# The second attention block put behind the first 24 products of the first MoE in TensorE's order

## The chip, the cores and the metric

The kernel runs on one core of a Trainium2 chip. The metric is the device time of one execution in microseconds; less is better. The times shown are medians over several executions, and the profile is of one further execution.

## What is computed

Attention with a decay over four batches, eight heads, 576 positions and a head dimension of 64, then two feed-forward layers over the 2304 tokens, all in float32 precision. The reference, cut to what matters:

```python
scores = matmul(q, k.T) / sqrt(64)
cum = cumsum(log(clip(f, 1e-4, 1)), -1)
scores = where(causal, -1e9, scores + cum[..., :, None] - cum[..., None, :])
attn = softmax(scores)                    # over keys, with 1e-9 in the divisor
x = matmul(attn, v) -> [2304, 512]        # tokens by heads*dim
h = x @ w_in                              # [512, 2048]
x = maximum(0.01 * h, h) @ w_out          # [2048, 512]
return ((x @ w_a) * (x @ w_b)) @ w_out2   # 512 -> 1536 -> 512
```

## The kernel before, in words

The attention runs in eight blocks (b, r): for batch b, r = 0 takes the first 256 queries and r = 1 the last 320. Each block goes through its eight heads in pairs. For the first batch, TensorE transposes queries and keys (tq, tk; ScalarE copies them out as qn, kn), makes the scores (s, and s4 for the last 64 queries), VectorE adds the decay and takes the maximum (p, line 320), ScalarE takes the exponential (line 291), TensorE transposes the result (pp; ScalarE copies it out as ph) and multiplies it with the values (av). The output is normalised (xn), transposed once more (px), and split into a high part xh (ScalarE) and a low part xl (VectorE) that are the input of the first MoE layer.

The first MoE layer goes over chunks of 256 tokens, and in each over eight pairs of 128 features. `l1(i, pr)` makes 24 products for chunk i and pair pr: two feature tiles, four slices of the model dimension, and three products each (high by high, high by low, low by high), into one PSUM tile `h`. For all chunks but the last two there is one such PSUM tile; the av and px of the first attention block use it too. ScalarE then reads it twice (gh and hs, the activation), VectorE makes gl = hs − gh, and `l2` makes 24 products into the two tiles `y`. `work(i, pr)` calls `l1` and then the `l2` of the pair before it.

The weights come from HBM as pairs of 32-bit words of doubles. For each 128-wide piece (wi_0 to wi_15 of w_in, wo_0 to wo_15 of w_out) `load_weight` issues one DMA on SP's queue into a raw buffer, of which there are two; then ScalarE takes the absolute value (L94), VectorE assembles a float in four steps (L95, L96, L97, L100; L97 and L100 read the raw buffer), ScalarE rounds it to the high part (L87), and VectorE subtracts to get the low part (L88).

The kernel is written in Tile. A scheduler orders the instructions of every engine by its own estimate of when each is ready and by priorities; the order in which the code is written sets the priorities, and `tc.high_priority` moves some ahead. The whole order of every engine is fixed before the kernel runs. The first block of attention (`att_steps(0)`) is written first, then the first two pieces of work of chunk 0 with a high priority, then the second block (`att_steps(1)`, the last 320 queries of batch 0) with loads and more work of chunk 0 between its steps. The names of the rows below carry these indices: s_0_1_0_2 is a score of block (0, 1), head 0, key tile 2; h_0_1 is chunk 0, pair 1; c_wi_6 and raw_wi_6 belong to the load of wi_6.

Of the kernel before, what the change touches and what calls it, by code (L numbers as in the profile page):

```python
# [26 lines left out]
def kernel(  # L27
# [13 lines left out]
    nc = tc.nc  # L41
# [5 lines left out]
    NF1, NF2, ND = F1 // P, F2 // P, DM // P  # L47
# [34 lines left out]
    def f32(ap):  # L82
        return ap.bitcast(F32)
# [77 lines left out]
    def x_chunk(c):  # L161
        if c not in xh:
            pool, bufs = (late["p"], 1) if c % 3 == 2 else (mp, 2)
            xh[c] = pool.tile([P, HP, T1], F32R, tag="xh", bufs=bufs, name=f"xh_{c}")
            xl[c] = pool.tile([P, HP, T1], F32R, tag="xl", bufs=bufs, name=f"xl_{c}")
        return xh[c], xl[c]
# [390 lines left out]
    def load_a(fi):  # L557
        wa[fi] = (
            *load_weight(wpool, stage, cols(w_in, fi), f"wi_{fi}", 512, 2, bufs=4 * NF1),
            *load_weight(wpool, stage, rows(w_out, fi), f"wo_{fi}", 512, 2, bufs=4 * NF1),  # L560
        )

    def l1(i, pr):
        ch, cl = x_chunk(i)
        last = i >= NB1 - 2
        hps = (pools["ps_ab"] if last else ps_y).tile(
            [P, 2, T1], F32, tag="ab0" if last else "h", bufs=2 if last else 1, name=f"h_{i}_{pr}"
        )
        for u in range(2):
            wih, wil = wa[2 * pr + u][0], wa[2 * pr + u][1]  # L570
            n = 0
            for c in reversed(range(ND)):
                for w, x in ((wih, ch), (wih, cl), (wil, ch)):
                    nc.tensor.matmul(  # L574
                        hps[:, u, :], w[:, c * P : c * P + P], x[:, c, :], start=(n == 0), stop=(n == 3 * ND - 1)
                    )
                    n += 1

        hs = mp.tile([P, 2, T1], F32, tag="hs", name=f"hs_{i}_{pr}")
        gh = mp.tile([P, 2, T1], F32R, tag="gh", name=f"gh_{i}_{pr}")  # L580
        gl = mp.tile([P, 2, T1], F32R, tag="gl", name=f"gl_{i}_{pr}")
        with tc.high_priority(offset=1):
            nc.scalar.activation(gh, hps, AF.Prelu, alpha=0.01)
            nc.scalar.activation(hs, hps, AF.Prelu, alpha=0.01)
        with tc.high_priority(offset=400 if last else 0):
            nc.vector.tensor_tensor(out=gl, in0=hs, in1=f32(gh), op=ALU.subtract)  # L586
        return gh, gl
# [3 lines left out]
    def l2(i, pr, gh, gl):  # L591
        if pr == 0:
            pool, tag, bufs = (pools["ps_ab"], "ab1", 2) if i == NB1 - 1 else (ps_y, "y", 2)
            ybank[i] = [pool.tile([P, 2, T1], F32, tag=tag, bufs=bufs, name=f"y_{i}_{z}") for z in range(2)]
        for u in range(2):
            fi = 2 * pr + u
            woh, wol = wa[fi][2], wa[fi][3]
            for d in range(ND):
                o = ybank[i][d // 2][:, d % 2, :]
                for n, (w, g) in enumerate(((woh, gh), (woh, gl), (wol, gh))):  # L600
                    nc.tensor.matmul(  # L601
                        o, w[:, d * P : d * P + P], g[:, u, :],
                        start=(fi == 0 and n == 0 and d % 2 == 0),
                        stop=(fi == NF1 - 1 and n == 2 and d % 2 == 1),
                    )
        if pr == NF1 // 2 - 1:
            for z in range(2):
                yo = mp.tile([P, 2, T1], F32, tag="hs", name=f"yo_{i}_{z}")
                nc.scalar.copy(yo, ybank[i][z])
                nc.scalar.dma_start(  # L610
                    y_dram[2 * z : 2 * z + 2, :, i * T1 : i * T1 + T1].rearrange("u p t -> p u t"), yo
                )
# [74 lines left out]
    def att_steps(n):  # L687

        if n == 0:

            sts = [{} for _ in range(H)]
            scores = [att_scores(*blocks[n], h, sts[h]) for h in range(H)]
            values = [att_values(*blocks[n], h, sts[h]) for h in range(H)]
            before = None
            for h in range(0, 2):
                next(scores[h])
            for h in range(0, H, 2):
                for z, _ in enumerate(beside(beside(*scores[h : h + 2]), before)):
                    if z == 3:
                        for g in scores[h + 2 : h + 4]:  # L700
                            next(g)
                    yield
                before = chain(*values[h : h + 2])
            yield from before
            return
        second = None
        for h in range(H):
            st = {}
            yield from beside(att_scores(*blocks[n], h, st), second)
            second = att_values(*blocks[n], h, st)  # L710
            if h % 2 == 1 and blocks[n][1] == 1:
                second = chain(second, att_last(blocks[n][0], h // 2, st["rec4"]))
        yield from second

    def chain(a, b):
        yield from a
        yield from b

    def beside(a, b):
        while a or b:  # L720
            for g in (a, b):
                if g and next(g, "end") == "end":
                    if g is a:
                        a = None
                    else:
                        b = None
                else:
                    if g:
                        yield
# [3 lines left out]
    def work(i, fi):  # L733
        pend.append((i, fi, *l1(i, fi)))
        if len(pend) > 1:
            l2(*pend.pop(0))


    zero, one = ([(i, fi) for fi in range(NF1 // 2)] for i in range(2))
    loaded = 0  # L740

    def load_next():
        nonlocal loaded
        if loaded < NF1:
            load_a(loaded)
            loaded += 1
# [7 lines left out]
        load_next()  # L754
    with tc.high_priority(offset=2000):
        work(*zero.pop(0))
        work(*zero.pop(0))
    for s, _ in enumerate(att_steps(1)):
        if s % 8 == 7:
            load_next()  # L760
        if s % 16 == 15 and 2 * (NF1 // 2 - len(zero)) + 2 <= loaded:
            work(*zero.pop(0))
    while zero:
        load_next()
        load_next()
# [80 lines left out]
```

## Time and profile before

| what | value |
|---|---|
| median of 3 runs | 1111.56 us (1110.79 to 1111.98) |
| profiled execution | 1109.59 us |
| its span (first to last instruction) | 1107.8 us |
| mean granted clock of TensorE | 0.989 of full speed |
| busy share of the span: TensorE, VectorE, ScalarE, GpSimd | 97%, 55%, 49%, 18% |

The profiled execution is 1.97 us under the median of the runs. Of its own time 1.8 us lie outside the span. Busy time is that of instructions only: an engine that waits is idle, and one that works at a lower clock is busy for longer. The profile lists for each group of instructions the idle time ahead of it and what ended that.

### The profile page before, as it was taken

Reading aid. Unit: us, or ns where it says so; the run is one execution under the profiler, and the core shown is the slowest. Engines: PE = TensorE matmul, PEld = TensorE weight load, DVE = VectorE, ACT = ScalarE, POOL = GpSimd, SP = SyncE. Lnnn points to the kernel's source line nnn. Section 1 sums busy time; section 2 is a strip of 40 time slices with the busy share of each in tenths; the row PEclk is TensorE's granted clock in tenths of the full one; section 3 lists DMA queues with packets and bytes.
Section 4 is the critical chain, followed back from the end, with each engine's and each line's share of the span. In section 5 each row is a group of like instructions: output and inputs, shape, how many; then the busy total and the mean of one; then the engine's idle time right before and its main releaser. Section 6 shows DMA issues by size and latency. Waiting matters only on the chain.

```text
span 1107.8 us, 19615 instructions
## 1 busy us (share of the span) xinstructions
PE 1079.2 (97%) x7021; PEld 967.2 (87%) x7021; DVE 614.0 (55%) x1484; ACT 543.2 (49%) x1257; POOL 204.5 (18%) x434
## 2 busy tenths in 40 slices
PE   5899999999999999999999999999999999999998
PEld 3577779999999999999999997888888888888897
DVE  5869887887777777677478877412111211211122
ACT  4656668878787878768554454312111211211121
POOL 4423322434243432333000000102001000100000
PEclk9879999999999999999999999999999999999999
DMA  7645545442452334422054454202000100100010
GB/s 196 195 130 172 159 120 103 96 94 48 79 124 62 94 58 83 109 62 53 9 165 144 142 152 152 76 1 76 1 1 20 48 1 1 48 1 1 1 39 20
DMA packets 185729, 86.77 MB, mean 78 GB/s; under 512 B 143840, under 2 KB 173536, under 8 KB 185632
## 3 DMA queue, kind: packets, MB, share of 16 engines
q1 hardware_dynamic: 180736, 80.80, 28.6%
q10 hardware_dynamic: 4896, 4.72, 1.3%
q8 instruction: 56, 0.92, 0.4%
q14 instruction: 41, 0.34, 0.1%
HBM read 75.96 MB, written 9.51 MB: 77 GB/s over the span
## 4 chain that ended last, share of the span: by engine, by line
PE 72%; DMA 11%; DVE 8%; ACT 4%; issue 3%; SPq 1%; POOL 0%; ACTq 0%; DVEq 0%; POOLq 0%
PE ab L653 25%; PE o L676 13%; PE h L574 11%; PE y L601 10%; PE s L76 5%; PE av L76 5%; PE pp L76 3%; DMA raw_wa<-in_moe_w_a_dram 3%; DMA raw_wb<-in_moe_w_b_dram 2%; DMA raw_wc<-in_moe_w_out_dram 1%; DMA xq<-in_q_dram 1%; DMA cumb<-cum_dram 1%; DMA raw_wi<-in_moe_w_in_dram 1%; DMA raw_wo<-in_moe_w_out_dram 1%; DMA sy<-y_dram 1%
## 5 line engine op out<-in xcount | busy, mean ns | idle before, releaser
L659 DVE TENSOR_TENSOR p<-ab,p 128x512 f32<-128x512 f32 (+1 forms) x60 | 38.3, 638 | 274.6 <-PE ab L653 272.0
L574 PE MATMUL h<-xh,wi_hi 128*128 128x256 f32 x576 | 164.6, 286 | 1.2 <-ACT wi_hi L87 1.2
L574 PE MATMUL h<-xh,wi_lo 128*128 128x256 f32 x576 | 164.1, 285 | 0.9 <-DVE wi_lo L88 0.9
L574 PE MATMUL h<-xl,wi_hi 128*128 128x256 f32 x576 | 164.3, 285 | 0.0
L601 PE MATMUL y<-gl,wo_hi 128*128 128x256 f32 x576 | 161.7, 282 | 1.0 <-DVE gl L586 1.0
L601 PE MATMUL y<-gh,wo_lo 128*128 128x256 f32 x576 | 161.1, 282 | 0.0
L601 PE MATMUL y<-gh,wo_hi 128*128 128x256 f32 x576 | 159.4, 282 | 0.0
L658 ACT COPY p<-ab 128x512 f32<-128x512 f32 (+1 forms) x60 | 32.7, 544 | 169.1 <-PE ab L653 168.7
L574 PEld LDWEIGHTS h<-xh,wi_hi 128*128 128x128 f32 x576 | 109.8, 191 | 5.2 <-issue 2.3
L574 PEld LDWEIGHTS h<-xh,wi_lo 128*128 128x128 f32 x576 | 109.8, 191 | 2.5 <-DVE wi_lo L88 1.1
L601 PEld LDWEIGHTS y<-gl,wo_hi 128*128 128x128 f32 x576 | 108.4, 188 | 2.9 <-DVE gl L586 1.6
L574 PEld LDWEIGHTS h<-xl,wi_hi 128*128 128x128 f32 x576 | 109.8, 191 | 0.8 <-issue 0.4
L601 PEld LDWEIGHTS y<-gh,wo_lo 128*128 128x128 f32 x576 | 108.3, 188 | 1.7 <-issue 1.2
L601 PEld LDWEIGHTS y<-gh,wo_hi 128*128 128x128 f32 x576 | 107.3, 188 | 1.8 <-issue 0.8
L313 POOL TENSOR_SCALAR p<-cumb,ncum_t 128x384 f32<-128x384 f32 (+1 forms) x112 | 75.1, 678 | 162.4 <-PE pp L76 47.8
L87 ACT CAST pph<-p 128x512 fp32r<-128x512 f32 (+1 forms) x60 | 34.8, 580 | 126.3 <-DVE p L659 126.2
L291 ACT ACTIVATE p<-p,stat 128x384 f32<-128x384 f32 (+4 forms) x128 | 77.0, 603 | 34.5 <-DVE stat L320 27.2
L88 POOL TENSOR_TENSOR yl<-sy,yh 128x512 fp32r<-128x512 f32 (+1 forms) x16 | 19.2, 1211 | 393.7 <-ACT yh L87 393.6
L653 PE MATMUL ab<-yh,wb_hi 128*128 128x512 f32 (+1 forms) x240 | 88.3, 368 | 0.9 <-DVE p L659 0.6
L653 PE MATMUL ab<-yh,wa_hi 128*128 128x512 f32 (+1 forms) x240 | 88.1, 367 | 0.0
L653 PE MATMUL ab<-yh,wa_lo 128*128 128x512 f32 (+1 forms) x240 | 88.1, 367 | 0.0
L653 PE MATMUL ab<-yl,wa_hi 128*128 128x512 f32 (+1 forms) x240 | 88.1, 367 | 0.0
(168 smaller groups left out, 2612.6 us busy)
## 6 DMA issues: line engine op xcount, KB each, us to landing
cumb<-cum_dram SPq DMA_DIRECT2D x32, 288.0 KB, 3.9
raw_wi<-in_moe_w_in_dram SPq DMA_DIRECT2D x16, 512.0 KB, 4.0
raw_wo<-in_moe_w_out_dram SPq DMA_DIRECT2D x16, 512.0 KB, 4.0
raw_wa<-in_moe_w_a_dram SPq DMA_DIRECT2D x12, 512.0 KB, 3.5
raw_wb<-in_moe_w_b_dram SPq DMA_DIRECT2D x12, 512.0 KB, 3.5
raw_wc<-in_moe_w_out_dram SPq DMA_DIRECT2D x12, 512.0 KB, 3.6
xq<-in_q_dram SPq DMA_DIRECT2D x144, 32.0 KB, 2.0
y_dram<-yo ACTq DMA_DIRECT2D x18, 256.0 KB, 3.0
```

Source lines behind the costliest of these rows:

```text
L76: return method(*args, **kw)
L87: nc.scalar.copy(hi, src)
L88: (lo_engine or nc.gpsimd).tensor_tensor(out=lo, in0=src, in1=f32(hi), op=ALU.subtract)
L291: act_att.activation(pt, pt, AF.Exp, bias=stat[:, 0, s : s + 1], scale=-1.0, accum_out=stat[:, 1, s : s + 1])
L313: pool_att.tensor_scalar(pt, cumb[:, :n], 1.0, ncum_t[:, t, bh : bh + 1], op0=ALU.mult, op1=ALU.add)
L574: nc.tensor.matmul(hps[:, u, :], w[:, c * P : c * P + P], x[:, c, :], start=(n == 0), stop=(n == 3 * ND - 1))
L601: nc.tensor.matmul(o, w[:, d * P : d * P + P], g[:, u, :], start=(fi == 0 and n == 0 and d % 2 == 0), stop=(fi == NF1 - 1 and n == 2 and d ...
L653: nc.tensor.matmul(o[:, :tn], w[:, c * P : c * P + P], y[:, c, :tn], start=(m == 0), stop=(m == 3 * ND - 1))
L658: nc.scalar.copy(p[:, :tn], ab[0][:, :tn])
L659: nc.vector.tensor_tensor(out=p[:, :tn], in0=ab[1][:, :tn], in1=p[:, :tn], op=ALU.mult)
L676: nc.tensor.matmul(o, g[:, t * P : t * P + P], w, start=(fi == 0 and m == 0), stop=(fi == NF2 - 1 and m == 2))
```

## The change

The last product that `l1` issues is remembered in `end[0]`. After the first `work` of chunk 0 this is the last of the first 24 products, h_0_0. Everything that the following loop traces on TensorE, that is the second attention block and the work of chunk 0 that is written between its steps, is then placed in a context (`tc.issue_after`) that lets no TensorE instruction stand ahead of it in TensorE's order.

```diff
+    end = [None]
+
     def l1(i, pr):
...
-                    nc.tensor.matmul(
+                    end[0] = nc.tensor.matmul(
                         hps[:, u, :], w[:, c * P : c * P + P], x[:, c, :], start=(n == 0), stop=(n == 3 * ND - 1)
                     )
...
     with tc.high_priority(offset=2000):
         work(*zero.pop(0))
+        first_end = end[0]
         work(*zero.pop(0))
-    for s, _ in enumerate(att_steps(1)):
-        if s % 8 == 7:
-            load_next()
-        if s % 16 == 15 and 2 * (NF1 // 2 - len(zero)) + 2 <= loaded:
-            work(*zero.pop(0))
+    with tc.issue_after(first_end.ins if hasattr(first_end, "ins") else first_end):
+        for s, _ in enumerate(att_steps(1)):
+            if s % 8 == 7:
+                load_next()
+            if s % 16 == 15 and 2 * (NF1 // 2 - len(zero)) + 2 <= loaded:
+                work(*zero.pop(0))
```

The count of instructions on every engine stays the same. The scheduler orders all engines anew around this, so three orders show what moves.

The first place is TensorE around the first 24 products. Before, the rows ahead of them are these (tq, tk and pp are transposes, s and s4 scores; h_0_0 is the first MoE product):

```order
L76 MATMUL s_0_1_0_2_741<-kn_0_1_0_709,qn_0_1_0_708 128x384
L76 MATMUL s_0_1_0_3_750<-kn_0_1_0_709,qn_0_1_0_708 128x512
L76 MATMUL px_0_0_7_614<-ident_65,xn_0_0_7_587 128x128 x2
L76 MATMUL s4_0_1_0_0_760<-kn_0_1_0_709,qn_0_1_0_708 64x288
L76 MATMUL pp_0_1_0_0_807<-ident_65,p_0_1_0_2_736 128x128 x3
L76 MATMUL s4_0_1_0_1_763<-kn_0_1_0_709,qn_0_1_0_708 64x288
L76 MATMUL pp_0_1_0_1_813<-ident_65,p_0_1_0_3_745 128x128 x4
L76 MATMUL tq_0_1_2_935<-ident_65,xq_0_1_2_925 128x128 x2
L76 MATMUL tq_0_1_2_935<-ident_65,xk_0_1_2_926 128x64
L76 MATMUL tk_0_1_2_0_940<-ident_65,xk_0_1_2_926 128x128 x2
L76 MATMUL s_0_1_1_2_803<-kn_0_1_0_709,qn_0_1_0_708 128x384
L574 MATMUL h_0_0_619<-xh_0_309,wi_0_hi_185 128x256
```

After the change px_0_0_7 is followed at once by the 24 products, and these are the rows around their last one:

```order
L576 MATMUL h_0_0_619<-xl_0_310,wi_1_hi_260 128x256
L576 MATMUL h_0_0_619<-xh_0_309,wi_1_lo_261 128x256
L76 MATMUL tq_0_1_0_720<-ident_65,xq_0_1_0_710 128x128 x2
L76 MATMUL tq_0_1_0_720<-ident_65,xk_0_1_0_711 128x64
L76 MATMUL tk_0_1_0_0_725<-ident_65,xk_0_1_0_711 128x128 x2
L76 MATMUL tk_0_1_0_2_729<-ident_65,xk_0_1_0_711 128x128 x2
L76 MATMUL tk_0_1_0_2_729<-ident_65,xk_0_1_0_711 128x64
L603 MATMUL y_0_0_681<-gh_0_0_645,wo_0_hi_197 128x256
L603 MATMUL y_0_1_682<-gh_0_0_645,wo_0_hi_197 128x256
L576 MATMUL h_0_1_650<-xh_0_309,wi_2_hi_332 128x256
```

Before, the scores of the first two heads stood ahead of the first MoE products; now even the first transposes of the second block stand behind them, and its first scores behind h_0_1.

The second place is ScalarE around the activation of the first 24 products (gh_0_0, hs_0_0). Before:

```order
L94 ACTIVATE c_wo_5_0_548<-raw_wo_5_0_546 128x512
L218 COPY kn_0_1_2_924<-tk_0_1_2_0_940 128x256
L87 CAST wi_5_hi_532<-c_wi_5_0_536 128x512
L291 ACTIVATE p_0_1_1_2_798,stat_0_1_0_707<-p_0_1_1_2_798,stat_0_1_0_707 128x384
L583 ACTIVATE gh_0_0_645<-h_0_0_619 128x512
L584 ACTIVATE hs_0_0_644<-h_0_0_619 128x512
L94 ACTIVATE c_wi_6_0_594<-raw_wi_6_0_592 128x512
```

After the change:

```order
L94 ACTIVATE c_wi_5_0_536<-raw_wi_5_0_534 128x512
L76 CAST xh_0_309<-px_0_0_7_614 128x256
L94 ACTIVATE c_wo_5_0_548<-raw_wo_5_0_546 128x512
L87 CAST wi_5_hi_532<-c_wi_5_0_536 128x512
L94 ACTIVATE c_wi_6_0_594<-raw_wi_6_0_592 128x512
L87 CAST wo_5_hi_544<-c_wo_5_0_548 128x512
L585 ACTIVATE gh_0_0_645<-h_0_0_619 128x512
L586 ACTIVATE hs_0_0_644<-h_0_0_619 128x512
L208 ACTIVATE qn_0_1_0_708<-tq_0_1_0_720 128x320
L218 COPY kn_0_1_0_709<-tk_0_1_0_0_725 128x256
```

The activation now stands behind L94 of c_wi_6, which before came after it, and the copies qn and kn of the second block stand behind the activation.

The third place is VectorE around the first softmax of the second block (p_0_1_0_2). Before:

```order
L76 TENSOR_TENSOR xn_0_0_7_587<-av_0_0_7_580,rec_0_0_7_577 128x2x64 x2
L100 SCALAR_TENSOR_TENSOR c_wo_4_0_489<-raw_wo_4_0_487,c_wo_4_0_489 128x512
L320 ISA p_0_1_0_2_736,stat_0_1_0_707<-s_0_1_0_2_741,p_0_1_0_2_736 128x384
L320 ISA stat_0_1_0_707 128x1
L95 TENSOR_SCALAR c_wi_5_0_536<-c_wi_5_0_536 128x512
```

After the change:

```order
L95 TENSOR_SCALAR c_wo_6_0_606<-c_wo_6_0_606 128x512
L96 TENSOR_SCALAR c_wo_6_0_606<-c_wo_6_0_606 128x512
L88 TENSOR_TENSOR wi_6_lo_591<-c_wi_6_0_594,wi_6_hi_590 128x512
L97 SCALAR_TENSOR_TENSOR c_wo_6_0_606<-raw_wo_6_0_604,c_wo_6_0_606 128x512
L320 ISA p_0_1_0_2_736,stat_0_1_0_707<-s_0_1_0_2_741,p_0_1_0_2_736 128x384
L320 ISA stat_0_1_0_707 128x1
```

The softmax has moved behind the conversions of wi_5, wo_5, wi_6 and most of wo_6, and xn_0_0_7, which stood ahead of the last step of c_wo_4, now stands behind it.

## Rows read from the trace of the kernel before

**Rows 1.** Busy time, share of the span and instructions of each engine.

```profile
PE 1079.2 (97%) x7021; PEld 967.2 (87%) x7021; DVE 614.0 (55%) x1484; ACT 543.2 (49%) x1257; POOL 204.5 (18%) x434
```

**Rows 2.** Windows, all engines: stretch, length, busy (count), PEclk, DMA share, GB/s.

```profile
core 0: us, PE busy (x) PEld busy (x) DVE busy (x) ACT busy (x) POOL busy (x), PEclk, DMA share, GB/s
55.00:83.00 28.00, 27.59 (x144) 19.69 (x143) 18.70 (x47) 15.38 (x34) 6.54 (x9) 0.78 0.48 128
```

**Rows 3.** Windows of PE alone: stretch, length, busy (count), PEclk, DMA share, GB/s.

```profile
54.00:66.00 12.00, 11.98 (x37) 0.50 0.67 179
68.00:158.00 90.00, 89.16 (x603) 1.00 0.56 155
158.00:166.00 8.00, 5.75 (x34) 0.80 0.19 31
```

**Rows 4.** Timeline of PE: start, us, instruction, count, [idle before and its releaser].

```profile
52.65 2.40 PE L76 MATMUL s<-kn,qn 64*128 64x384 f32 x4
54.98 0.69 PE L76 MATMUL px<-ident,xn 128*128 128x128 f32 x2
55.60 1.22 PE L76 MATMUL s<-kn,qn 64*64 64x288 f32 x2
...
62.78 0.58 PE L574 MATMUL h<-xh,wi_hi 128*128 128x256 f32 x1
...
67.82 1.12 PE L76 MATMUL s<-kn,qn 64*128 64x512 f32 x2
...
70.56 0.28 PE L574 MATMUL h<-xh,wi_hi 128*128 128x256 f32 x1
...
73.24 0.28 PE L574 MATMUL h<-xh,wi_lo 128*128 128x256 f32 x1
...
161.10 0.39 PE L574 MATMUL h<-xh,wi_hi 128*128 128x256 f32 x1 [1.15 <-ACT wi_hi L87]
...
162.76 0.50 PE L574 MATMUL h<-xh,wi_lo 128*128 128x256 f32 x1 [0.92 <-DVE wi_lo L88]
```

**Rows 5.** Timeline of DVE around the conversions and the first scores.

```profile
53.42 0.69 DVE L100 SCALAR_TENSOR_TENSOR c_wo<-raw_wo,c_wo 128x512 int32<-128x512 int32 x1
54.02 0.56 DVE L320 CUSTOM_DVE_ANT_0 p<-s,p 128x384 f32<-128x384 f32 x1
...
55.70 0.43 DVE L95 TENSOR_SCALAR c_wi<-c_wi 128x512 f32<-128x512 f32 x1 [1.11 <-ACT c_wi L94]
...
57.97 0.41 DVE L76 TENSOR_TENSOR xl<-px,xh 128x256 fp32r<-128x256 f32 x1
58.30 0.67 DVE L97 SCALAR_TENSOR_TENSOR c_wi<-raw_wi,c_wi 128x512 int32<-128x512 int32 x1
...
63.00 0.56 DVE L320 CUSTOM_DVE_ANT_0 p<-s,p 128x384 f32<-128x384 f32 x1 [2.95 <-PE s L76]
...
69.09 0.69 DVE L320 CUSTOM_DVE_ANT_0 p<-s,p 128x512 f32<-128x512 f32 x1 [2.80 <-PE s L76]
```

**Rows 6.** Timeline of ACT around the loads and the first activations.

```profile
55.01 0.66 ACT L94 ACTIVATE c_wi<-raw_wi 128x512 f32<-128x512 f32 x1 [3.20 <-DMA raw_wi<-in_moe_w_in_dram]
55.57 0.60 ACT L87 CAST wo_hi<-c_wo 128x512 fp32r<-128x512 f32 x1
...
56.69 0.35 ACT L76 CAST xh<-px 128x256 fp32r<-128x256 f32 x1
...
67.93 0.60 ACT L583 ACTIVATE gh<-h 128x512 fp32r<-128x512 f32 x1 [3.62 <-PE h L574]
68.42 0.59 ACT L584 ACTIVATE hs<-h 128x512 f32<-128x512 f32 x1
...
75.16 0.66 ACT L94 ACTIVATE c_wo<-raw_wo 128x512 f32<-128x512 f32 x1 [3.44 <-DMA raw_wo<-in_moe_w_out_dram]
75.73 0.58 ACT L583 ACTIVATE gh<-h 128x512 fp32r<-128x512 f32 x1
```

**Rows 7.** Timeline of SP's queue: the loads of wi_5 and wi_6.

```profile
50.85 0.37 SPq L114 DMA_DIRECT2D raw_wi<-in_moe_w_in_dram  x1
...
61.39 0.40 SPq L114 DMA_DIRECT2D raw_wi<-in_moe_w_in_dram  x1
```

## The prediction

> **What bounds the kernel now.** The busy line of the page comes first: TensorE is busy 97% of the span, VectorE 55% [rows 1]. So the time can change through TensorE's idle time, through the clock granted to it, or through the work, and the work stays: no instruction is added or removed. The windows come next. TensorE is busy 27.59 of 28.00 us in 55 to 83 [rows 2]; over 68 to 158 it lacks less than 1 of 90 us and holds the full clock (1.00), while in 158 to 166 it lacks 2.25 of 8 us [rows 3]. TensorE's timeline names that place: the last pair of the first chunk waits 1.15 us for the cast of a weight and 0.92 us for its low part, which VectorE makes [rows 4]. [...]
>
> The other loss is a clock that is low while TensorE has work: 54 to 66 is busy for 11.98 of 12.00 us at 0.50 [rows 3]. That stretch holds scores, transposes and the first products of the first MoE.
>
> **The change, part by part.** Each term is a moment that shifts; the moments of the changed kernel are worked out from durations of rows.
>
> 1. *When the first 24 products (h0) begin.* They need the last piece of input: px (0.69 [rows 4]), xh on ScalarE, xl on VectorE. Before, px ran at 54.98 behind scores, and h0 at 62.78 behind more of the second block [rows 4]. Now px needs only xn, and xn stands on VectorE behind the L100 that ended near 54.1 before [rows 5]; with fewer rows ahead I put px at 54.1 to 54.8. On ScalarE xh stands behind L94 of wi_5, which waits for a transfer: issued at 50.85, L94 at 55.01, so 4.16 [rows 6, 7]. I put the issue 0.2 later, since SP's queue is filled anew: L94 at 55.2, xh 55.75, xl 56.1, done 56.5 (steps from [rows 5, 6]). **h0 begins at 56.5**, 6.3 earlier. Before, it took from 62.78 to 67.8, mostly at the lower clock [rows 3, 4]; as long again, a little less, ends it at 61 to 61.6. Five transposes of the second block follow, to 62.4.
>
> 2. *The new wait.* There is one PSUM tile for h, so the second 24 products (h1) begin when ScalarE has read h0 twice (gh, hs). In ScalarE's order gh now stands behind L94 of wi_6 and a cast. L94 of wi_6 waits for its transfer, and that is issued when VectorE has done L95, L96, L97 and L100 of wi_5: with xl between them 2.3 to 2.6 us from 55.75 (0.43, as much again, 0.67, 0.69 and 0.41 [rows 5]), so 58.1 at the earliest, and three more issues on SP's queue (0.40 each [rows 7]) make it 59.4. With 4.16 to land L94 starts at 62.3 to 63.6. Then L94 (0.56 to the next row), cast (0.5), gh (0.49) and hs (0.59) [rows 6]: h1 at 64.4 to 65.8, **taken at 64.5**, because a transfer of a weight mostly goes out as soon as its buffer is free. Without this hold-up gh runs at 61.4 and h1 starts at 62.5. Behind gh on ScalarE stand qn and kn of the second block, for which its scores wait.
>
> That a row which waits for a DMA holds up the next one, whose input is there, the trace shows at 75.16: L94 waits 3.44 us for a DMA and gh follows at 75.73, though its products ended at 73.52 [rows 4, 6]. [...]
>
> 3. *Where that leaves TensorE.* h1 comes at 64.5 for 70.56 before [rows 4]. But by then the kernel before had done work that is now still to do: the first scores (52.65 to 54.98, with little of it slow: 1.9 at the full clock), all of 55.60 to 62.78 (7.18 at the lower level, 3.6 at the full one), and 67.82 to 70.56 without two y products (2.5) [rows 4]. Together 8.0. The like moment is 64.5 + 8.0 = 72.5: **1.9 late**.
>
> 4. *The clock after the new idle time.* TensorE stands 1.5 to 2 us idle before h1. The nearest row is the stall at 161 to 163, 2.07 us in two waits [rows 4], after which 1.6 us were lost to the clock [rows 3]. Bounds: 0 and 1.6. I take **0.8**, the middle, since the gap is about as long but transposes and two y products break it. [...]
>
> 5. *What comes back at 158 to 166.* VectorE has less to do ahead of the weights. The second block's scores need qn and kn (after hs, some 1.2 us) and on TensorE stand behind h1 (2.96 [rows 4]), so its first softmax moves from 54.02 [rows 5] to about 68.5. The waits of 2.95 and 2.80 us for scores that VectorE had at 60 and 66 [rows 5] go to conversions instead: 5.75 earlier for every later weight. The low part of the last one was there at 162.76 [rows 4], and so is at about 157; TensorE asked for that weight at 161.10 − 1.15 = 159.95 [rows 4], and by the terms above asks 2.7 later. So both waits go, and with them the slow clock: 2.25 + 1.6 = **3.85 back**.
>
> Sum: 1.9 + 0.8 − 3.85 = −1.15. In TensorE's order the number of switches between products of the two formats (fp32 and fp32r) goes from 269 to 281, at about 0.1 us each in the timeline's spacing: within the rounding. Further terms are taken as 0, since the last 1952 of 6873 products stand in the same order. The profiled execution took 1109.59, so 1108.5 by its measure; the median of the runs is 1.97 above it: **1110.5**.
>
> **Rivals.**
>
> *A. As worked out:* 1110.5; its own range is 1108.9 to 1112.8 (h1 at 65.8: +1.3; all of the clock's loss: +0.8; none: −0.8; waits before 158 covered a little more: −0.8).
>
> *B. ScalarE does not hold gh up.* If the transfer of wi_6 has landed when h0 ends (out by 57.4, or in 3 us), h1 comes at 62.5, 2.0 earlier, there is no gap and no clock to lose (0.8): −3.95, 1107.6. For it: DMA is loaded by 0.48 in 55 to 83 [rows 2], so a landing could be quicker than 4.16. Against it: 58.1 comes out of VectorE's own steps.
>
> *C. TensorE runs dry on the second block (slower).* Its softmax stands behind conversions that run ahead as far as their buffers let them, and its scores start some 14 us later, while chunk-0 products come no faster than their weights. Then TensorE waits between 64 and 168 for a softmax, and the 3.85 are moved, not won: 1.9 + 0.8 = +2.7, and 1.2 for switches, to 1114.4. It decides from about 3 us of idle time in 64 to 168. For it: it was just this block that filled TensorE between the pairs before (under 1 us idle in 90 [rows 3]). Against it: VectorE is busy 18.70 of 28 us in 55 to 83 [rows 2], so 9 us are free.
>
> *D. The wait for the last weight stays.* If its load is held by SP's order and not by VectorE's waits, the 2.25 and the clock stay, and 1.9 + 0.8 = +2.7 remain: 1113.2. For it: VectorE was mostly busy after 70; against it, the row at 162.76 waits for VectorE, not for a transfer [rows 4].
>
> **How the numbers follow.** About 0.2%, 2.2 us, is what a measurement of this kernel can tell from no change: faster is under 1109.3, slower over 1113.8. A has 55%, B 22%, C 18%, D 5%. A is within the bound but for a sixth under 1109.3 (0.09) and a little over 1113.8 (0.02); B is faster but for a fifth (0.18); C is slower, D within the bound but for a fifth (0.01). Together 0.27, 0.52, 0.21. The range reaches to B less 0.8 (1106.8), its h0 a little earlier, and to C with 0.6 more idle time (1115.0); what is left out is a dry stretch longer than C's and a gain in places that the rows don't show.
>
> **What would show it.** h0 at 56 to 57 in TensorE's timeline. gh behind an L94 that waits for raw_wi, and TensorE idle 1.5 to 2 us until h1 at 64.4 to 65.8. A granted clock below 1 after that gap, or not: the 0.8. No wait for wi_hi or wi_lo in 158 to 166, and a clock of 1.00 there. TensorE's idle time over 64 to 158 at about 1 us beside the gap; at 3 or more it is C. The prediction is wrong if TensorE's busy time changes by more than 4 us with the same instructions, or if the last pair still waits for its weight.

## The result, and the profile after

The changed kernel takes 1120.92 us (median of 6 runs, 1116.56 to 1123.0) for 1111.77 us before (6 runs): a ratio of 1.0079, 95% interval 1.0057 to 1.0101. It is 9 us slower; the forecast was 1110.5 us, with a range up to 1115.0.

The windows of TensorE in the profile after, first over the stretches of [rows 3] and then over the rest (stretch, length, busy and count, PEclk, DMA share, GB/s):

```profile
58.00:64.00 6.00, 5.80 (x27) 1.00 0.57 180
64.00:158.00 94.00, 93.35 (x603) 1.00 0.57 152
158.00:166.00 8.00, 8.00 (x62) 1.00 0.17 35
166.00:330.00 164.00, 158.49 (x1312) 1.00 0.41 83
330.00:560.00 230.00, 228.10 (x1898) 1.00 0.32 70
560.00:720.00 160.00, 155.42 (x1116) 1.00 0.45 137
```

The same stretches of the profile before, as far as [rows 3] does not have them:

```profile
64.00:158.00 94.00, 93.16 (x624) 0.98 0.55 153
166.00:330.00 164.00, 163.38 (x1362) 1.00 0.44 90
330.00:560.00 230.00, 229.47 (x1915) 1.00 0.31 69
560.00:720.00 160.00, 158.09 (x1099) 1.00 0.45 139
```

The reader is to see two things. The place on which the forecast put its gain came out as forecast: 158 to 166 is now busy for all of its 8 us, where 2.25 were idle before, and 64 to 158 has 0.65 us of idle time, not the 3 that rival C needed. The loss lies in places that the forecast set to nothing: 5.51 us idle in 166 to 330 for 0.62 before, 1.90 for 0.53 in 330 to 560, 4.58 for 1.91 in 560 to 720.

The early part in the timelines of the profile after, TensorE and ScalarE (answering to [rows 4, 6]):

```profile
58.20 0.58 PE L576 MATMUL h<-xh,wi_hi 128*128 128x256 f32 x1 [1.51 <-DVE xl L76]
58.58 0.42 PE L576 MATMUL h<-xl,wi_hi 128*128 128x256 f32 x1
58.79 0.42 PE L576 MATMUL h<-xh,wi_lo 128*128 128x256 f32 x1
...
65.66 0.51 PE L603 MATMUL y<-gh,wo_hi 128*128 128x256 f32 x2 [0.65 <-ACT gh L585]
66.15 0.39 PE L576 MATMUL h<-xh,wi_hi 128*128 128x256 f32 x1
66.37 0.28 PE L576 MATMUL h<-xl,wi_hi 128*128 128x256 f32 x1
66.49 0.28 PE L576 MATMUL h<-xh,wi_lo 128*128 128x256 f32 x1
```

```profile
63.93 0.67 ACT L94 ACTIVATE c_wi<-raw_wi 128x512 f32<-128x512 f32 x1 [2.74 <-DMA raw_wi<-in_moe_w_in_dram]
64.51 0.60 ACT L87 CAST wo_hi<-c_wo 128x512 fp32r<-128x512 f32 x1
65.02 0.59 ACT L585 ACTIVATE gh<-h 128x512 fp32r<-128x512 f32 x1
65.51 0.59 ACT L586 ACTIVATE hs<-h 128x512 f32<-128x512 f32 x1
```

The first 24 products begin at 58.20 (56.5 forecast) and the second 24 at 66.15 (64.5 forecast): 7.95 apart for 8.0. gh stands behind L94, which waits 2.74 us for its load, as forecast; of the gap on TensorE only 0.65 us is left, because the transposes of the second block take until 65.0 instead of 62.4.

Where TensorE waits in the later stretch, 166 to 330 us after (engine, line and what it waited for; us in total, times, longest):

```profile
PE h L576 <- ACT hs L586: 1.6, 2, 0.9
PE s L76 <- DVE stat L320: 1.5, 2, 1.1
PE h L576 <- ACT xh L373: 0.9, 1, 0.9
PE s L76 <- ACT p L330: 0.7, 1, 0.7
PE s L76 <- DVE st L361: 0.5, 1, 0.5
```

Half of it is the first MoE waiting (h), half attention (s), on two engines (VectorE and ScalarE). No one instruction is to blame, so the question became what all these waits have in common. The order of the program gives it. The table counts the MoE products (h and y) that stand ahead of a row in TensorE's order:

| row on TensorE | before | after | later by |
|---|---|---|---|
| s_0_1_0_2 (block (0, 1), the one that the change names) | 0 | 50 | 50 |
| s_1_0_2_0 (170 us) | 360 | 384 | 24 |
| s_1_0_7_0 | 549 | 584 | 35 |
| s_1_1_0_2 | 574 | 615 | 41 |
| s_1_1_7_2 | 912 | 945 | 33 |
| s_2_0_7_0 (330 us) | 1208 | 1255 | 47 |
| s_2_1_0_2 | 1272 | 1288 | 16 |
| s_3_0_0_0 | 1706 | 1714 | 8 |

The change puts one block behind 24 products. The scheduler then starts the following blocks later as well, up to block (3, 0). Below this is called the lag. It is not even: of all attention rows that stand between 170 and 330 us in the kernel before, single ones stand 4 products sooner and others up to 51 later, 23 later on average. From 330 to 400 us the average is 10; from 400 to 480 us attention stands 4 to 5 products sooner than before on average, and its last rows, near 551 us, stand 19 later again.

### The profile page after: what moved, and what is told of

It is laid out like the page before. It is cut to its first block, busy times and chain, and to the rows that moved or that the text cites. A ratio compares the mean times of both kernels' runs of the same rounds, so it can differ in the third digit from the quotient of the medians.

```text
span 1120.2 us, 19639 instructions
## 1 busy us (share of the span) xinstructions
PE 1079.8 (96%) x7021; PEld 967.0 (86%) x7021; DVE 613.5 (55%) x1484; ACT 541.6 (48%) x1257; POOL 205.6 (18%) x434
## 4 chain that ended last, share of the span: by engine, by line
PE 72%; DMA 12%; DVE 7%; ACT 4%; issue 2%; SPq 2%; POOL 0%; DVEq 0%; ACTq 0%; POOLq 0%
PE ab L655 23%; PE h L576 12%; PE o L678 12%; PE y L603 11%; PE s L76 5%; PE av L76 5%; PE pp L76 3%; DMA raw_wa<-in_moe_w_a_dram 2%; DMA raw_wi<-in_moe_w_in_dram 2%; DMA raw_wb<-in_moe_w_b_dram 2%; DMA cumb<-cum_dram 1%; DMA sy<-y_dram 1%; DMA y_dram<-yo 1%; DMA raw_wo<-in_moe_w_out_dram 1%; DMA xq<-in_q_dram 1%
## 5 line engine op out<-in xcount | busy, mean ns | idle before, releaser
L88 POOL TENSOR_TENSOR yl<-sy,yh 128x512 fp32r<-128x512 f32 (+1 forms) x16 | 19.1, 1208 | 395.7 <-ACT yh L87 391.8
L655 PE MATMUL ab<-yl,wb_hi 128*128 128x512 f32 (+1 forms) x240 | 88.2, 367 | 0.0
```

The lines of the kernel that those rows point to most:

```text
L88: (lo_engine or nc.gpsimd).tensor_tensor(out=lo, in0=src, in1=f32(hi), op=ALU.subtract)
L655: nc.tensor.matmul(o[:, :tn], w[:, c * P : c * P + P], y[:, c, :tn], start=(m == 0), stop=(m == 3 * ND - 1))
```

## The experiments

### Is it the order that was drawn anew behind 170 us, or a debt from the early part?

The order of an engine can be taken from another kernel, since both trace the same instructions under the same numbers. The edit, put at the end of the kernel, is this:

```diff
+    by = {i.name: i for i in nc.cur_bb.bb.instructions}
+    for chain_ in LATE_ORDER:
+        names = [f"I-{n}" for n in chain_ if f"I-{n}" in by]
+        for first_, next_ in zip(names, names[1:]):
+            tc.add_manual_dep(
+                by[next_], first_, mybir.DependencyInfo(mybir.DependencyClass.NoSync, mybir.DependencyReason.DATA), reason="pin"
+            )
```

The edges set the place in the queue and wait for nothing. LATE_ORDER holds one list per engine. Instructions traced ahead of chunk 1 are the early part, the rest the late part. The four runs take their lists as follows. The runs of this section were taken in several sessions, in which the median of the kernel before lay between 1111.64 and 1113.77 us. So versions are compared by their ratios, each to the kernel before in its own session, and a difference in us that is given for a ratio is worked out from it.

```diff
-    e1: all of the change as the scheduler orders it
+    e1: early part as after, late part as before
+    e2: early part as before, late part as after (without issue_after)
+    e3: early part and chunks 1 and 2 as after, the rest as before
+    e4: early part as after, chunks 1 to 6 as before, chunks 7 and 8 and the second MoE as after
```

> The change, with the instructions that are traced from chunk 1 of the first MoE on (chunk 1 to the end, and attention from block 3 on) put on every engine in the order that they have in the kernel before; what is traced ahead of that keeps the order of the change. Theory O (order): the change loses its time behind 170 us, because the scheduler gave the later blocks another order on every engine; then this takes back nearly all of it: 1109.5 to 1112.5 us. Rival D (debt): the second block's late softmax leaves VectorE and ScalarE behind, and TensorE pays for it later in whatever order the rest stands: 1118 to 1122 us.

> The mirror image: the kernel before with its own order up to chunk 1, and from there on the order of the change on every engine. No instruction of the second attention block is put behind the first 24 products. Theory O: 1118 to 1122 us, as slow as the change. Rival D: 1110 to 1113 us, as the kernel before.

> The change with its own order up to the third chunk of the first MoE (about 300 us), and the order of the kernel before from there on. Theory O: the losses that TensorE's timeline shows in 175 to 300 stay (4.7 us more than before), those behind go: 1114 to 1118 us. Rival D: 1118 to 1122 us.

> The change with its own order ahead of chunk 1, the order of the kernel before for chunks 1 to 6, and again its own order for chunks 7 and 8 and the second MoE (behind 560 us). Theory O: only the losses behind 560 us stay, 2.8 us of waits and about 1 us of work in 600 to 800: 1112 to 1116 us. Rival D: 1118 to 1122 us.

| run | median us | ratio to before | 95% interval |
|---|---|---|---|
| e1, change with late order of before | 1111.93 | 0.9982 | 0.9968 to 0.9996 |
| e2, before with late order of the change | 1124.12 | 1.0085 | 1.0061 to 1.0109 |
| e3, late order of the change up to 300 us | 1120.32 | 1.0056 | 1.0040 to 1.0072 |
| e4, late order of the change from 560 us | 1115.38 | 1.0007 | 0.9992 to 1.0022 |

Theory O holds and the debt falls, from both sides: the change without its late order is not slower but a little faster than before, and the kernel before with that late order is as slow as the change (its median, 1124.12, lies above the 1118 to 1122 that were expected). e3 and e4 say that both ends of the late part have a share: 0.74% and 0.25% over e1. e4 came out as expected; e3 did not: 1120.32 is outside the 1114 to 1118 of theory O. In e3 TensorE takes 144.8 us from the first product of chunk 2 to that of chunk 4, where the two orders meet, for 140.1 in the change, so the share that it gives to the first stretch is too large.

### Which engine's order?

```diff
-    e1: late part of all five engines as before
+    e9: late part of TensorE alone as before
```

> The change, with TensorE's rows from chunk 1 on in the order of the kernel before; ScalarE, VectorE, GpSimd and SP are left to the scheduler. Theory O in its narrow form (TensorE's order alone carries the loss, the others follow it): like the first experiment, 0.996 to 0.9995 of the time before. Rival (the other engines' order carries it): 1.003 or more.

e9 takes 1109.46 us, 0.9983 (0.9974 to 0.9992). With TensorE's order given, the scheduler puts the other engines almost as before by itself (against e1, 6 rows of VectorE, 2 of ScalarE and 10 of SP's queue have moved). So TensorE's order decides the loss, by itself or through the order that the other engines take from it. e9 is also the best version: it beats both kernels, by 1.9 us and by some 11. Its windows of TensorE:

```profile
158.00:166.00 8.00, 7.40 (x61) 1.00 0.17 34
166.00:330.00 164.00, 163.77 (x1362) 1.00 0.44 91
330.00:560.00 230.00, 230.00 (x1922) 1.00 0.31 70
560.00:720.00 160.00, 157.33 (x1086) 1.00 0.45 137
```

The idle time of 166 to 560 is gone (0.23 us), and what is left behind 560 is near that of before.

### Is it the lag, or particular places?

In TensorE's late order of before, attention rows (tq, s, pp, av, px) were moved back by a number of MoE products; the order within the MoE stays, and so does that within attention but for 4 to 25 rows where moved rows meet others.

```diff
-    e5, e6, e10: TensorE's late order as before
+    e5: every attention row 30 products further back
+    e6: every attention row 10 products further back
+    e10: attention rows of blocks (1, 0) and (1, 1) alone 30 products further back
```

> The kernel before, with one thing moved: in TensorE's order every attention row behind the first chunk stands 30 MoE products (h and y) further back; the other engines are ordered by the scheduler around that. In the change these rows stand 17 to 47 products further back between 170 and 330 us. Theory L (lag): this lag as such costs the time, because TensorE asks later for what ScalarE, VectorE and GpSimd have to work on, and waits for it at the places where attention is the longer chain: 6 to 12 us slower than before. Rival P (particular places): the lag is harmless, since a chunk needs attention only much later, and what costs are particular rows that the scheduler interleaved badly: within 2.5 us of before.

> The same with 10 products for 30. Theory L: 1 to 5 us slower than before, between before and the 30. Rival P: within 2.5 us of before.

> The kernel before, with attention blocks (1, 0) and (1, 1) alone 30 MoE products further back in TensorE's order; from block (2, 0) on (280 us) TensorE has the order of before again. Theory L: the loss is that of the stretch, 3 to 5 us as TensorE's timeline showed in 175 to 300 of the run with 30 throughout, and 0 to 3 more where the rows close up again: 3 to 8 us slower than before. Rival (the lag costs only behind 300 us, where the run with 30 throughout lost most): within 2 us of before.

| run | median us | ratio to before | 95% interval |
|---|---|---|---|
| e5, 30 back | 1124.97 | 1.0128 | 1.0100 to 1.0156 |
| e6, 10 back | 1117.70 | 1.0068 | 1.0040 to 1.0097 |
| e10, 30 back, to 280 us | 1120.72 | 1.0095 | 1.0078 to 1.0111 |

The lag costs, and more of it costs more; that it is harmless is out. But all three sizes were above what was expected: 30 products cost 14.2 us (6 to 12 expected), 10 cost 7.6 (1 to 5), and e10 lost 10.6 us (3 to 8), with most of its wait at one place, where the rows close up again:

```profile
PE s L90 <- DVE st L375: 4.7, 1, 4.7
PE h L588 <- ACT wi_hi L101: 1.3, 1, 1.3
PE pp L90 <- DVE xl L388: 1.1, 1, 1.1
```

These are TensorE's waits of e10 in 166 to 330; the 4.7 us stands ahead of the first score of block (2, 0), which now follows sooner on the rows of block (1, 1). e10 therefore says little of the lag as such. Of e6's loss more than half (4.8 of 8.1 us in the profiled executions) lies behind the start of chunk 7; that place is taken up below.

The edge drawn to another product was meant to give less late lag with more early shift:

```diff
-        first_end = end[0]
         work(*zero.pop(0))
+        first_end = end[47]
```

(end is a list of all products here.)

> The change with its edge drawn to the last of the first 48 products of the first MoE in place of the 24th, and everything ordered by the scheduler. The first scores of the second block now stand 96 products back in place of 50, but the attention behind 170 us only 24 at first, 12 to 24 up to 240 us and 5 or fewer from 260 us on. Theory L: the late loss is about half of the change's, 3 to 6 us slower than before. Rival S (the size of the early shift sets the price): 12 us or more slower than before. Rival P has no forecast here, since all places are new.

e7 takes 1124.80 us, 1.0119 (1.0090 to 1.0148): 13.2 us, beyond the 3 to 6 that theory L gave it and in the range of rival S (12 or more). So the late lag is not all that costs here. TensorE's idle time in e7 lies in several stretches (1.6 us of 90 in 68 to 158, 4.7 of 164 in 166 to 330, 4.0 of 160 in 560 to 720); which part of it the doubled early shift causes was not taken apart.

The last of this group keeps the lag of the change and takes away its particular interleaving:

```diff
-    e9: TensorE's late order as before
+    e12: the same, each attention row moved back by the change's lag, averaged over 60 rows on either side
+    e13: as e12, and the other engines from chunk 7 on as before
```

> As e9 (the change, TensorE's rows from chunk 1 on in the order of before, the rest left to the scheduler), but every attention row moved back by the lag that it has in the change, averaged over the 60 attention rows on either side: 12 to 33 MoE products between 170 and 330 us, 15 and fewer behind. So the change's lag is there and its particular interleaving is not (single rows stand 10 products, one standard deviation, from where the change has them). Theory L (the lag itself costs): 1.004 to 1.010 of the time before. Rival P (particular places cost, and in the runs with attention 10 and 30 back it was the places where rows were squeezed together): 0.998 to 1.002.

> As e12 (the change with the smoothed lag), but ScalarE, VectorE, GpSimd and SP have their rows of chunks 7 and 8 and of the second MoE (behind 560 us) in the order of before; TensorE's order is that of e12. If the lag costs only while it lasts (166 to 560 us; TensorE's timeline of e12 shows about 4 us more waits and slow stretches there than e9): 1.001 to 1.004 of the time before. If the order behind 560 us has no part in it: 1.004 to 1.009, as e12.

e12 takes 1120.03 us, 1.0062 (1.0037 to 1.0087): the smoothed lag alone brings back 0.79% of the 0.96% by which the change stands over e9. Particular places are left with the small rest. e13 takes 1119.96 us, 1.0052 (1.0034 to 1.0070), in the range that was expected if the order of the other engines behind 560 us has no part, and not told apart from e12.

### The end: what is late behind 560 us

In the change, and in e2, e4, e5, e7, e12 and e16, the last activation of chunk 8 stands on ScalarE behind a cast that waits for a transfer. That was the first suspect, with this edit:

```diff
-    ScalarE: c_wa_8, yh, gh_8_7, hs_8_7
+    ScalarE: c_wa_8, gh_8_7, hs_8_7, yh
```

> The change with one edit: on ScalarE the last activation of chunk 8 (gh, hs) stands ahead of the cast yh that waits 0.91 us for a transfer of the second MoE's input; all other rows of all engines stand as in the change. If that wait is a part of the loss: TensorE's wait of 1.37 us for gh at 670 goes or falls below 0.5, and the time is 0.5 to 2 us below the change: 1.0055 to 1.0078. If TensorE then waits for something else: 1.0075 to 1.0095 and the wait moves.

e14 takes 1121.85 us, 1.0078 (1.0057 to 1.0098): nothing is won. TensorE's wait for gh fell from 1.37 to 0.7 us, and two waits of 0.8 us of the second MoE's first products took its place. The wait for gh is a symptom.

What the runs whose attention ends late share is the time of the first load of the second MoE's weights (wa_0). It can go out when the attention's memory is released, and so it does, 0.1 us behind the last attention product. SP's queue and TensorE before:

```profile
551.89 0.37 SPq L114 DMA_DIRECT2D raw_wa<-in_moe_w_a_dram  x1
...
551.55 0.27 PE L76 MATMUL ppx<-ident,x 64*128 64x64 f32 x1
```

and after:

```profile
562.30 0.37 SPq L114 DMA_DIRECT2D raw_wa<-in_moe_w_a_dram  x1
...
561.95 0.27 PE L76 MATMUL ppx<-ident,x 64*128 64x64 f32 x1
```

Chunk 7 begins at 560.02 before and at 568.21 after, so the load has 8.1 us of lead before and 5.9 after. The two last runs make this end late alone on TensorE, and on time alone; the other engines are left to the scheduler:

```diff
-    e9: TensorE's late order as before
+    e16: the last 12 attention products 19 MoE products further back, all else on TensorE as e9
-    e12: smoothed lag throughout
+    e15: smoothed lag up to block (2, 1), attention from block (3, 0) on as before
```

> As e12 (the change with the smoothed lag), but attention rows from block (3, 0) on (about 405 us) stand where they stand before, so that attention ends on time. Theory E (attention's end sets when the second MoE's weights are loaded, and a late end costs waits for gl and gh behind 570 us): the first load goes out 8 us ahead of chunk 7, TensorE's idle time in the 150 us from chunk 7 on falls from 6.3 us in e12 to 2 to 3.5, and 1.000 to 1.004 of the time before is left for the lag between 166 and 400 us. Rival: 1.004 or more, the end does not matter.

> As e9 (the change, TensorE's late rows as before: 0.9983), with one edit: the last 12 attention products (the last 8 of av4_3_1_6, and ppx_3) stand 19 MoE products further back. Theory E: the first load of the second MoE goes out about 2.2 us later against chunk 7 (near 5.9 ahead for 8.1), TensorE's idle time in the 150 us from chunk 7 on rises from 2.7 to 4 to 6.5 us, and the time is 2 to 4 us above e9: 1.000 to 1.003 of before. Rival: as e9, 0.997 to 0.9995.

| run | median us | ratio to before | 95% interval | lead of the first load us | TensorE idle in 150 us from chunk 7 |
|---|---|---|---|---|---|
| before | 1111.77 | 1 | | 8.1 | 1.9 |
| e9 | 1109.46 | 0.9983 | 0.9974 to 0.9992 | 8.1 | 2.7 |
| e16, only the end late | 1115.34 | 1.0016 | 1.0001 to 1.0030 | 5.9 | 5.2 |
| e15, lag to 400 us, end on time | 1116.73 | 1.0026 | 1.0013 to 1.0039 | 8.1 | 2.6 |
| e4, end on time, other engines there as in the change | 1115.38 | 1.0007 | 0.9992 to 1.0022 | 8.1 | 5.8 |
| e13, lag throughout, other engines there as before | 1119.96 | 1.0052 | 1.0034 to 1.0070 | 5.9 | 6.6 |
| e12, lag throughout | 1120.03 | 1.0062 | 1.0037 to 1.0087 | 6.0 | 6.3 |
| change | 1120.92 | 1.0079 | 1.0057 to 1.0101 | 5.9 | 4.6 |

Twelve small products, moved by 2.2 us, cost 0.33% (3.7 us) over e9, and the intervals do not touch. What TensorE waits for in e16, from chunk 7 on, and its window (e9's is above):

```profile
PE y L617 <- DVE gl L602: 2.7, 4, 1.3
PE y L617 <- ACT gh L599: 2.4, 2, 2.1
```

```profile
560.00:720.00 160.00, 154.82 (x1061) 0.98 0.46 139
```

In e9 there is no wait for gh there, and 1.5 us for gl. Beside the 2.5 us of further idle time some 3 us of this execution went to the clock: 0.98 of 160 us for 1.00 in e9. It read 0.74 over 630 to 636 (4.43 us busy) and 0.80 over 660 to 666 (4.00 us busy); that the waits there brought it down is not shown. The conversions of the second MoE's weights run on VectorE and ScalarE, in whose queues gl and gh stand among them, so a conversion that waits for its load holds them up, as L94 with its wait of 2.74 us does with gh at 63.93 after the change: at 628.08 in e16 ScalarE has waited 3.07 us for a load of wa, and at 632.73 TensorE has waited 1.33 us for gl.

But e16 moves more than the load. The scheduler drew the end of both engines anew around it: 61 rows of VectorE and 50 of ScalarE stand elsewhere than in e9, whose end is row for row that of before; e12 has the same new order, e15 that of before. The late load and the new order are told apart by two other runs of the table. In e13 the load is late and the other engines have the order of before there (to within 3 rows): TensorE idles as long as in e12. In e4 the load is on time and the order is the change's: TensorE idles 5.8 us as well. So either is enough for the waits; how much of the 3.7 us each of them has in e16 is not shown. The end alone (0.33%) and the lag up to 400 us alone (0.43%) add up to e12's 0.79%, within the intervals.

### The hold-up on ScalarE (term 2 of the forecast)

```diff
-    ScalarE: c_wi_6 (L94, waits for its load), wo_5_hi, gh_0_0, hs_0_0
+    ScalarE: gh_0_0, hs_0_0, c_wi_6, wo_5_hi
```

> The change with the late order of before (as in the first experiment), and on ScalarE the activation of the first 24 products (gh, hs) put ahead of the step L94 that waits for the load of wi_6. My term 2 (that L94 holds the activation up): in the change gh ran at 65.02, 1.5 us behind the end of the products; here it runs within 0.5 us of that end, the second 24 products begin 0.8 to 1.2 us sooner, and the time is 0 to 1.5 us below that of the first experiment, so 2 to 3.5 us faster than before. Rival: the transposes of the second block keep TensorE busy until then anyway, and nothing comes sooner by more than 0.3 us.

> As e9, with the activation of the first 24 products (gh, hs) ahead of the step L94 that waits for the load of wi_6 on ScalarE. Theory (term 2 is real and reaches the end): the second 24 products come 1.2 us sooner against the first than in e9, as the trace of e8 showed, and the time is 0.5 to 1.5 us below e9. Rival: no difference to e9 beyond the interval, since TensorE's clock or a later wait takes it back.

e8 (late order as e1) takes 1111.11 us, 0.9999 (0.9980 to 1.0018); e11 (late order as e9) takes 1110.05 us, 0.9998 (0.9983 to 1.0012), no better than e9. The first step is as expected: from the start of the first 24 products to that of the second it is 6.78 us in e11 and 7.80 in e9. TensorE of e11:

```profile
56.91 0.58 PE L590 MATMUL h<-xh,wi_hi 128*128 128x256 f32 x1 [1.35 <-DVE xl L90]
...
63.69 0.28 PE L590 MATMUL h<-xh,wi_hi 128*128 128x256 f32 x1
...
148.30 0.51 PE L617 MATMUL y<-gh,wo_hi 128*128 128x256 f32 x2 [0.76 <-ACT gh L599]
```

Up to the pair 5 of chunk 0 e11 is 0.9 us ahead of e9, and by pair 7 it is 1.0 behind. TensorE waits 1.2 us on the way, 0.8 of it for gh, and the loads went out no earlier than in e9 (the last but one at 141.76 for 140.31). That the weights pace chunk 0, so that TensorE cannot run ahead of them, fits this. It is not shown apart, since around the swap the scheduler also put the last four loads two to four places further back in SP's queue.

## Why the prediction was wrong, point by point

**The step that failed** is the sentence "Further terms are taken as 0, since the last 1952 of 6873 products stand in the same order". The equal tail was taken for an answer about everything between it and the early part. Between 170 and 690 us most rows of TensorE had moved, the lag among them, and the forecast read that the order changed there only as a count of switches between formats. e1, e2 and e9 show that this term is not 0 but +0.96%, 10.7 us.

**Terms 1 to 5**, the early part, were right in sum: forecast −1.15 us, and e9, in which only they are left, measures −1.9 us (−2.9 to −0.9), e1 −2.0. Part of that is luck, since a clock loss that was counted did not come (term 4) and the idle time ahead of h1 was shorter (term 2). Term 1: h0 began 1.7 later than forecast in the change's profile, but over ten profiles with the same early order it lies between 55.62 and 58.20 (56.70 in e9), so the 56.5 is within what the start of the kernel varies by. Term 2: the hold-up was there, but its idle time 0.65 us for the 1.5 to 2 forecast. Term 4: no stretch at the lower spacing follows that gap; products stand 0.12 us apart from 66.4 on, so its price was 0, not 0.8. Term 5: the waits for the last weight are gone, as forecast, and with that rival D is out. The slow clock that it counted with 1.6 us stands in the profile before (162 to 163 reads 0.94, 163 to 166 reads 0.50) and not in that after, where 158 to 166 reads 1.00.

**Rival B** did not come: ScalarE does hold gh up. Putting gh ahead of it (e11) didn't give its 2 us either.

**Rival C** had the right victim, attention that runs late against the MoE, and the right sign. It was wrong in the place (64 to 168 has hardly any idle time) and so in its price: it looked at the block that was moved, and the blocks behind it lost the time. The prices of C and D are also added to the wrong base: +2.7 and +1.2 were put on the forecast of 1110.5 in place of the 1111.56 of before, so C comes to 1115.5 and D to 1114.3. With C's own sum put right the range would have ended near 1116.1, still under the 1120.92 measured.

**What stays open**: the change is 0.17% above e12, which could be particular places or the interval. e7 is dearer than the lag explains, and why is not shown. In e4 the late order from 560 us on costs 0.25% over e1 although the first load has its 8.1 us of lead, so the order of VectorE and ScalarE there can do the same harm as a late start; which rows of it do was not taken apart beyond e14. An order with attention further forward than before was not tried.

## What to carry to other kernels

Where a scheduler sets the order, an edge at one place shifts all that is ordered later: compare where rows of one stream stand against the other (here attention against MoE products) over the whole program, and price every stretch in which they moved, not only the one that the edit names. Here a stream that was started later stayed later for some 250 us, and what hangs on its end, the release of memory that starts the next loads, was late too. When an early gain is wanted without that, keep the late order by edges, as e9 does.

## What was not expected of the hardware

After the change the PEclk column misses a lower clock. It reads 1.00 in 58 to 64 us, but the products there start 0.21 us apart, as in the stretch before that reads 0.50 [rows 3], for 0.12 from 66.37 on. Two products of that stretch before:

```profile
63.16 0.41 PE L574 MATMUL h<-xl,wi_hi 128*128 128x256 f32 x1
63.37 0.41 PE L574 MATMUL h<-xh,wi_lo 128*128 128x256 f32 x1
```

In e8 the clock fell with 0.35 us of idle time ahead of it. Its TensorE:

```profile
137.09 0.91 PE L90 MATMUL s<-kn,qn 64*128 64x384 f32 x2 [0.35 <-ACT kn L232]
```

```profile
139.00:158.00 19.00, 19.00 (x102) 0.73 0.45 104
```

The only wait from 130 us on is the 0.35 us at 137. The engine then worked on fp32 products of attention for 3 us, and from 140 to 150 the clock read 0.50: products of the first MoE start 0.21 us apart from 145.96 to 148.74 and 0.12 apart from 150.45 on. The engine was busy for all 19.00 us of the window, and by its reading of 0.73 a share of 0.27, some 5 us, went. What brought the clock down is not shown: e11 has the same order on TensorE and reads 1.00 from 130 to 158. The loss is as much as e8's profiled execution is longer than its median (5.1 us).
